# A fixed software-pipelined order for the attention stage, with its weights loaded by casting transfers, in a sigmoid-attention plus feed-forward kernel

**Chip, cores, metric.** One core of a Trainium2 chip. The metric is the device time of one launch in microseconds (us); lower is better. Every time below is a median of fast runs unless said otherwise.

## The reference

```
scores = q @ k.T / sqrt(64) - log(448)            # 8 batches, 12 heads, 448 tokens, head size 64
x = (sigmoid(scores) @ v), heads put side by side  # 3584 tokens x 768
h = x @ w_in                                       # 768 -> 2048
out = (h * sigmoid(beta * h)) @ w_out              # 2048 -> 768
```

No softmax: each score goes through a sigmoid alone, so attention is two matrix products with an elementwise function between.

## The kernel before

Weights are staged in float32 and cast on VectorE at the start. Then 48 units (a batch and a pair of heads) of attention, written in plain order; the framework's scheduler decides the order on each engine. Names: `qn`, `kn`, `vn` as loaded; `tpq`, `tpk` transposes in PSUM; `scc` scores in PSUM, `at2` sigmoids, `av` values in PSUM, `xT` the result.

```python
for c in range(CK):                          # first weights; w_out the same way, 16 pieces
    stage = spool.tile([128, FF], FP32, ...)
    nc.sync.dma_start(out=stage, in_=moe_w_in[c * 128:(c + 1) * 128, :])
    nc.vector.tensor_copy(out=w_in_sb[c], in_=stage)
for b in range(B):
    for hp in range(NHP):
        ...                                  # load qn, kn (GpSimd, casting to fp16), vn (Sync)
        nc.vector.tensor_copy(out=vnh, in_=vn)
        for c in range(NC):                  # 4 transposes of q, copy; then 4 of k, copy
            nc.tensor.transpose(tpq[:, c, :], qn[:, c, :, :], ident)
        ...
        for c in range(NC):                  # two matmuls on the two halves of the array's rows
            scc = sc_ps_pool.tile([SC, 2, 512], FP32, ...)           # two buffers
            for hh in range(2):
                nc.tensor.matmul(out=scc[:, hh, :S], lhsT=kT[lo:lo + 64, c, :], rhs=qT[lo:lo + 64, :], ...)
            nc.scalar.activation(out=at2[:, :, c, :], in_=scc[:, :, :S], func=SIG, ...)
        av = av_ps_pool.tile([128, 2, 512], FP32, ...)               # one buffer
        for c in range(NC):                  # two matmuls on the two halves of its columns
            for hh in range(2):
                nc.tensor.matmul(out=av[lo:lo + 64, hh, :S], lhsT=vnh[:, hh, c, :], rhs=at2[:, hh, c, :], ...)
        for hh in range(2):
            nc.vector.tensor_copy(out=xT_sb[hp][lo:lo + 64, ...], in_=av[lo:lo + 64, hh, :S])
# then the feed-forward stage, unchanged: hps matmuls, sigmoid, product, ops matmuls, store
```

Of the kernel before, what the change touches and what calls it, by code (L numbers as in the profile page):

```python
# [15 lines left out]
def kernel(  # L16
# [10 lines left out]
    nc = tc.nc  # L27
# [27 lines left out]
    with nc.allow_non_contiguous_dma("beta gather"):  # L55
        nc.sync.dma_start(out=beta_sb, in_=moe_beta.rearrange("(m p) -> p m", p=128))

    xT_sb = [wpool.tile([128, NT], FP16, name=f"xT{c}", tag=f"xT{c}")
             for c in range(CK)]

    with tc.tile_pool(name="stage", bufs=2) as spool:
        w_in_sb = []
        for c in range(CK):
            stage = spool.tile([128, FF], FP32, name="wi_stage", tag="wi_stage")
            nc.sync.dma_start(out=stage, in_=moe_w_in[c * 128:(c + 1) * 128, :])
            t = wpool.tile([128, FF], FP16, name=f"w_in_sb{c}", tag=f"wi{c}")
            nc.vector.tensor_copy(out=t, in_=stage)
            w_in_sb.append(t)
        w_out_sb = []
        for m in range(MF):  # L70
            stage = spool.tile([128, DM], FP32, name="wo_stage", tag="wo_stage")
            nc.sync.dma_start(out=stage, in_=moe_w_out[m * 128:(m + 1) * 128, :])
            t = wpool.tile([128, DM], FP16, name=f"w_out_sb{m}", tag=f"wo{m}")
            nc.vector.tensor_copy(out=t, in_=stage)
            w_out_sb.append(t)

        with tc.tile_pool(name="a_sb", bufs=2) as apool, \
                tc.tile_pool(name="tp_ps", bufs=1, space=bass.MemoryType.PSUM) as tp_ps_pool, \
                tc.tile_pool(name="sc_ps", bufs=2, space=bass.MemoryType.PSUM) as sc_ps_pool, \
                tc.tile_pool(name="av_ps", bufs=1, space=bass.MemoryType.PSUM) as av_ps_pool:  # L80
            for b in range(B):
                for hp in range(NHP):
                    h0 = 2 * hp
                    qn = apool.tile([SC, NC, 2, D], FP16, name="qn", tag="qn")
                    kn = apool.tile([SC, NC, 2, D], FP16, name="kn", tag="kn")
                    vn = apool.tile([SC, 2, NC, D], FP32, name="vn", tag="vn")
                    for t, src in ((qn, q), (kn, k)):
                        nc.gpsimd.dma_start(  # L88
                            out=t,
                            in_=src[b, h0:h0 + 2].rearrange(  # L90
                                "hh (p j) d -> p j hh d", j=NC),
                        )
                    nc.sync.dma_start(
                        out=vn,
                        in_=v[b, h0:h0 + 2].rearrange("hh (p j) d -> p hh j d",
                                                      j=NC),
                    )
                    vnh = apool.tile([SC, 2, NC, D], FP16, name="vnh", tag="vnh")
                    nc.vector.tensor_copy(out=vnh, in_=vn)
                    qT = apool.tile([128, S], FP16, name="qT", tag="qT")  # L100
                    kT = apool.tile([128, NC, SC], FP16, name="kT", tag="kT")
                    tpq = tp_ps_pool.tile([128, NC, SC], FP16, name="tpq", tag="tpq")
                    for c in range(NC):
                        nc.tensor.transpose(tpq[:, c, :], qn[:, c, :, :], ident)  # L104
                    nc.vector.tensor_copy(  # L105
                        out=qT.rearrange("f (p c) -> f c p", c=NC), in_=tpq)
                    tpk = tp_ps_pool.tile([128, NC, SC], FP16, name="tpk", tag="tpk")
                    for c in range(NC):
                        nc.tensor.transpose(tpk[:, c, :], kn[:, c, :, :], ident)  # L109
                    nc.vector.tensor_copy(out=kT, in_=tpk)  # L110
                    at2 = apool.tile([SC, 2, NC, S], FP16, name="at2",
                                     tag="at2", bufs=2)
                    for c in range(NC):
                        scc = sc_ps_pool.tile([SC, 2, 512], FP32, name="scc",
                                              tag="scc")
                        for hh in range(2):
                            lo = hh * 64
                            nc.tensor.matmul(  # L118
                                out=scc[:, hh, :S],
                                lhsT=kT[lo:lo + 64, c, :],  # L120
                                rhs=qT[lo:lo + 64, :],
                                start=True, stop=True,
                            )
                        nc.scalar.activation(  # L124
                            out=at2[:, :, c, :], in_=scc[:, :, :S], func=SIG,
                            bias=neglog[:SC], scale=scale,
                        )
                    av = av_ps_pool.tile([128, 2, 512], FP32, name="av",
                                         tag="av")
                    for c in range(NC):  # L130
                        for hh in range(2):
                            lo = hh * 64
                            nc.tensor.matmul(  # L133
                                out=av[lo:lo + 64, hh, :S],
                                lhsT=vnh[:, hh, c, :],
                                rhs=at2[:, hh, c, :],
                                start=(c == 0), stop=(c == NC - 1),
                            )
                    for hh in range(2):
                        lo = hh * 64  # L140
                        nc.vector.tensor_copy(  # L141
                            out=xT_sb[hp][lo:lo + 64, b * S:(b + 1) * S],
                            in_=av[lo:lo + 64, hh, :S])

    with tc.tile_pool(name="m_sb", bufs=2) as mpool, \
            tc.tile_pool(name="g_sb", bufs=2 * MF) as gpool, \
            tc.tile_pool(name="h_ps", bufs=2, space=bass.MemoryType.PSUM) as h_ps_pool, \
            tc.tile_pool(name="o_ps", bufs=2, space=bass.MemoryType.PSUM) as o_ps_pool:
        for g in range(NG):
            t0 = g * TGRP  # L150
            gts = []
            for m in range(MF):
                hps = h_ps_pool.tile([128, NTC, 512], FP32, name="hps", tag="hps")
                for c in range(CK):
                    for n in range(NTC):
                        nc.tensor.matmul(  # L156
                            out=hps[:, n, :S],
                            lhsT=w_in_sb[c][:, m * 128:(m + 1) * 128],
                            rhs=xT_sb[c][:, t0 + n * S:t0 + (n + 1) * S],
                            start=(c == 0), stop=(c == CK - 1),  # L160
                        )
                sg = mpool.tile([128, NTC, S], FP32, name="sg", tag="sg")
                nc.scalar.activation(  # L163
                    out=sg, in_=hps[:, :, :S], func=SIG,
                    bias=0.0, scale=beta_sb[:, m:m + 1],
                )
                gt = gpool.tile([128, TGRP], FP16, name="gt", tag="gt")
                nc.vector.tensor_tensor(  # L168
                    out=gt.rearrange("p (n x) -> p n x", x=S),
                    in0=hps[:, :, :S], in1=sg, op=mybir.AluOpType.mult,  # L170
                )
                gts.append(gt)
            for tt in range(TT):
                ops = o_ps_pool.tile([128, DM], FP32, name="ops", tag="ops")
                for m in range(MF):
                    st = gts[m][:, tt * 128:(tt + 1) * 128]
                    nc.tensor.matmul(out=ops[:, 0:512], lhsT=st,  # L177
                                     rhs=w_out_sb[m][:, 0:512],
                                     start=(m == 0), stop=(m == MF - 1))
                    nc.tensor.matmul(out=ops[:, 512:DM], lhsT=st,  # L180
                                     rhs=w_out_sb[m][:, 512:DM],
                                     start=(m == 0), stop=(m == MF - 1))
                osb = mpool.tile([128, DM], FP32, name="osb", tag="osb")
                nc.scalar.copy(out=osb, in_=ops)  # L184
                nc.sync.dma_start(
                    out=out[t0 + tt * 128: t0 + (tt + 1) * 128, :], in_=osb)
# [30 lines left out]
```

## Time and profile before

| | before |
|---|---|
| time | 585.02 us (583.67 to 587.31) |
| attention, until the first `hps` matmul | 283.2 us of a span of 582.5 |
| one unit in mid-attention | 5.46 us |
| feed-forward | 299.2 us |
| TensorE / ScalarE busy | 95% / 48% |

The prediction shows the lines these come from. In a line of the page's groups, the columns are line, engine, operation, tiles and shapes, count, busy us and mean ns of one, then idle time before and what ended most of it.

### The profile page before, as it was taken

The page shows a single profiled execution, that of the slowest core. Times are in us where ns is not written, and L with a number is a line of the kernel's source. Part 1 is how long each engine was busy: PE and PEld are TensorE (multiplying, and loading weights), DVE is VectorE, ACT ScalarE, POOL GpSimd, SP SyncE. Part 2 cuts the span into 40 slices and gives each one's busy share as a digit, 9 for nine tenths or more (in the row PEclk, how much of TensorE's full clock was granted, in tenths as well). Part 3 has the DMA queues.
Part 4 walks back from the last instruction along what each step waited for, and adds up shares of the span by engine and source line. Part 5 has one row for each costly group of instructions (what it writes and reads, how often), then busy time and mean ns, then how long its engine had stood idle before and what let it go on. Part 6 is the DMA issues. An engine that isn't in the chain of part 4 may idle for free.

```text
span 582.5 us, 6912 instructions
## 1 busy us (share of the span) xinstructions
PE 554.1 (95%) x2816; PEld 255.2 (44%) x2816; DVE 232.9 (40%) x328; ACT 277.7 (48%) x285; POOL 111.4 (19%) x102
## 2 busy tenths in 40 slices
PE   1479999999999999999999999999999999999996
PEld 0233333333333333333355555555655556555564
DVE  2678755555555555555344101441004410044100
ACT  1456776776776776777544112441124421244211
POOL 5425443344344344340000000000000000000000
PEclk9999999999999999999999999999999999999999
DMA  9999977977977977972000111001120001200022
GB/s 251 335 259 217 199 79 81 95 76 83 96 78 81 94 78 82 95 79 34 0 1 0 55 73 64 1 1 55 55 82 0 1 36 73 82 0 1 28 81 82
DMA packets 108367, 46.07 MB, mean 79 GB/s; under 512 B 91184, under 2 KB 101936, under 8 KB 107568
## 3 DMA queue, kind: packets, MB, share of 16 engines
q0 software_dynamic: 87552, 11.02, 29.7%
q1 hardware_dynamic: 20784, 34.62, 18.0%
q8 instruction: 22, 0.36, 0.3%
q14 instruction: 9, 0.07, 0.0%
HBM read 45.62 MB, written 11.01 MB: 97 GB/s over the span
## 4 chain that ended last, share of the span: by engine, by line
PE 93%; DMA 5%; issue 1%; DVE 1%; ACT 0%; POOL 0%; POOLq 0%; ACTq 0%
PE hps L156 26%; PE av L133 18%; PE scc L118 17%; PE ops L177 17%; PE ops L180 8%; PE tpk L109 4%; PE tpq L104 4%; DMA qn<-in_q_dram 3%; DMA kn<-in_k_dram 2%; DVE xT L141 1%; ACT at L124 0%; ACT osb L184 0%; POOL qn L88 0%; POOL ident masks.py:197 0%; POOLq L88 0%
## 5 line engine op out<-in xcount | busy, mean ns | idle before, releaser
L124 ACT ACTIVATE at<-scc,neglog 112x896 f16<-112x896 f32 x192 | 189.5, 1007 | 90.9 <-PE scc L118 82.0
L156 PE MATMUL hps<-xT,w_in_sb 128*128 128x448 f16 x768 | 149.7, 353 | 0.0
L177 PE MATMUL ops<-w_out_sb,gt 128*128 128x512 f16 x448 | 145.8, 379 | 0.0
L168 DVE TENSOR_TENSOR gt<-hps,sg 128x896 f16<-128x896 f32 x64 | 69.9, 1092 | 189.3 <-ACT sg L163 189.3
L180 PE MATMUL ops<-w_out_sb,gt 128*128 128x256 f16 x448 | 122.1, 273 | 0.0
L118 PE MATMUL scc<-qT,kT 64*112 64x448 f16 x384 | 117.9, 615 | 3.4 <-ACT at L124 3.1
L133 PE MATMUL av<-at,vnh 112*64 112x448 f16 x384 | 115.9, 580 | 0.6 <-DVE xT L141 0.4
L156 PEld LDWEIGHTS <-w_in_sb 128*128 128x128 f16 x768 | 74.8, 98 | 74.2 <-issue 6.9
L163 ACT ACTIVATE sg<-hps,beta_sb 128x896 f32<-128x896 f32 x64 | 64.5, 1007 | 86.8 <-PE hps L156 86.8
L141 DVE CAST xT<-av 64x448 f16<-64x448 f32 x96 | 59.7, 622 | 67.7 <-PE av L133 67.1
L184 ACT COPY osb<-ops 128x768 f32<-128x768 f32 x28 | 22.4, 799 | 122.6 <-PE ops L180 122.6
L88 POOL DMA_DIRECT2D qn<-in_q_dram x48 | 56.4, 1175 | 123.7 <-PE tpq L104 110.7
L105 DVE COPY qT<-tpq 128x448 f16<-128x448 f16 x48 | 55.4, 1153 | 36.2 <-PE scc L118 36.1
L118 PEld LDWEIGHTS <-kT 64*112 64x112 f16 x384 | 32.5, 166 | 80.3 <-issue 79.5
L177 PEld LDWEIGHTS <-gt 128*128 128x128 f16 x448 | 43.8, 98 | 52.6
L88 POOL DMA_DIRECT2D kn<-in_k_dram x48 | 58.2, 1213 | 25.4 <-PE tpk L109 17.9
L133 PEld LDWEIGHTS <-vnh 112*64 112x64 f16 x384 | 29.5, 141 | 53.7 <-issue 52.9
L180 PEld LDWEIGHTS <-gt 128*128 128x128 f16 x448 | 43.8, 98 | 5.6
L104 PE MATMUL tpq<-ident,qn 112*128 112x112 f16 x192 | 26.9, 294 | 16.9 <-DMA qn<-in_q_dram 16.4
L109 PE MATMUL tpk<-ident,kn 112*128 112x112 f16 x192 | 35.0, 294 | 3.0 <-DMA kn<-in_k_dram 2.9
L104 PEld LDWEIGHTS <-qn 112*128 112x128 f16 x192 | 15.6, 132 | 34.6 <-DMA qn<-in_q_dram 17.5
L109 PEld LDWEIGHTS <-kn 112*128 112x128 f16 x192 | 17.6, 131 | 21.6 <-issue 16.9
(13 smaller groups left out, 61.3 us busy)
## 6 DMA issues: line engine op xcount, KB each, us to landing
vn<-in_v_dram SPq DMA_DIRECT2D x48, 224.0 KB, 3.0
out_dram<-osb SPq DMA_DIRECT2D x28, 384.0 KB, 2.3
wi_stage<-in_moe_w_in_dram SPq DMA_DIRECT2D x6, 1024.0 KB, 6.6
wo_stage<-in_moe_w_out_dram SPq DMA_DIRECT2D x16, 384.0 KB, 4.1
qn<-in_q_dram POOLq DMA_DIRECT2D x48, 112.0 KB, 3.5
kn<-in_k_dram POOLq DMA_DIRECT2D x48, 112.0 KB, 4.2
beta_sb<-in_moe_beta_dram SPq DMA_DIRECT2D x1, 8.0 KB, 3.0
```

Source lines behind the costliest of these rows:

```text
L88: nc.gpsimd.dma_start(out=t, in_=src[b, h0:h0 + 2].rearrange("hh (p j) d -> p j hh d", j=NC),)
L104: nc.tensor.transpose(tpq[:, c, :], qn[:, c, :, :], ident)
L109: nc.tensor.transpose(tpk[:, c, :], kn[:, c, :, :], ident)
L118: nc.tensor.matmul(out=scc[:, hh, :S], lhsT=kT[lo:lo + 64, c, :], rhs=qT[lo:lo + 64, :], start=True, stop=True,)
L124: nc.scalar.activation(out=at2[:, :, c, :], in_=scc[:, :, :S], func=SIG, bias=neglog[:SC], scale=scale,)
L133: nc.tensor.matmul(out=av[lo:lo + 64, hh, :S], lhsT=vnh[:, hh, c, :], rhs=at2[:, hh, c, :], start=(c == 0), stop=(c == NC - 1),)
L141: nc.vector.tensor_copy(out=xT_sb[hp][lo:lo + 64, b * S:(b + 1) * S], in_=av[lo:lo + 64, hh, :S])
L156: nc.tensor.matmul(out=hps[:, n, :S], lhsT=w_in_sb[c][:, m * 128:(m + 1) * 128], rhs=xT_sb[c][:, t0 + n * S:t0 + (n + 1) * S], start=(c == ...
L163: nc.scalar.activation(out=sg, in_=hps[:, :, :S], func=SIG, bias=0.0, scale=beta_sb[:, m:m + 1],)
L168: nc.vector.tensor_tensor(out=gt.rearrange("p (n x) -> p n x", x=S), in0=hps[:, :, :S], in1=sg, op=mybir.AluOpType.mult,)
L177: nc.tensor.matmul(out=ops[:, 0:512], lhsT=st, rhs=w_out_sb[m][:, 0:512], start=(m == 0), stop=(m == MF - 1))
L180: nc.tensor.matmul(out=ops[:, 512:DM], lhsT=st, rhs=w_out_sb[m][:, 512:DM], start=(m == 0), stop=(m == MF - 1))
```

## The change

The intent: keep TensorE on a fixed order in which transposes run two units early and values one unit late, load three units ahead, and take the weights out of the start. GpSimd loads the weights during attention with transfers that cast, so the staging and 22 casts on VectorE go. The values of both heads share one PSUM tile of 128 x 512 (two buffers), so one copy of 128 partitions takes the place of two of 64 (622 ns each before).

```diff
+    with ..., tc.manual_schedule(engines={mybir.EngineType.PE, mybir.EngineType.Pool}):
+        load(0); load(1); load(2)
+        transposes(0); transposes(1)
+        for n in range(NI):
+            scores(n, 0)
+            values(n - 1, (0, 1))
+            scores(n, 1)
+            transposes(n + 2)
+            load(n + 3)
+            scores(n, 2)
+            values(n - 1, (2, 3))
+            scores(n, 3)
+            if n % 6 == 5 and n // 6 < CK:
+                nc.gpsimd.dma_start(out=w_in_sb[c], in_=moe_w_in[...])     # 1 MB, casts
+        values(NI - 1, (0, 1, 2, 3))
+        for m in range(MF):
+            nc.gpsimd.dma_start(out=w_out_sb[m], in_=moe_w_out[...])
-    # staging of w_in and w_out over Sync, 22 casts on VectorE
-    # the loops over b and hp shown above
```

## The prediction

> **What bounds the kernel now.** I read the page's busy row, slices and chain, then the busy time by stage, then the chain in a window of the middle, then the timeline of single runs of matmuls.

> From the page:

> ```profile
> PE 554.1 (95%) x2816; PEld 255.2 (44%) x2816; DVE 232.9 (40%) x328; ACT 277.7 (48%) x285; POOL 111.4 (19%) x102
> ...
> PE hps L156 26%; PE av L133 18%; PE scc L118 17%; PE ops L177 17%; PE ops L180 8%; PE tpk L109 4%; PE tpq L104 4%; DMA qn<-in_q_dram 3%; DMA kn<-in_k_dram 2%; DVE xT L141 1%; ACT at L124 0%; ACT osb L184 0%; POOL qn L88 0%; POOL ident masks
> ...
> L124 ACT ACTIVATE at<-scc,neglog 112x896 f16<-112x896 f32 x192 | 189.5, 1007 | 90.9 <-PE scc L118 82.0
> L118 PE MATMUL scc<-qT,kT 64*112 64x448 f16 x384 | 117.9, 615 | 3.4 <-ACT at L124 3.1
> L133 PE MATMUL av<-at,vnh 112*64 112x448 f16 x384 | 115.9, 580 | 0.6 <-DVE xT L141 0.4
> L141 DVE CAST xT<-av 64x448 f16<-64x448 f32 x96 | 59.7, 622 | 67.7 <-PE av L133 67.1
> ```

> The chain is TensorE nearly throughout. The kernel has two stages: attention (48 units, each one batch and a pair of heads) until 283.2 us, then the feed-forward part. Stages (the columns are length, busy time and count by engine, granted clock, DMA share, GB/s):

> ```profile
> 60.00:258.00 198.00, 198.00 (x874) 69.79 (x871) 112.60 (x186) 143.48 (x146) 81.90 (x72) 1.00 0.85 92
> 283.20:582.40 299.20, 294.82 (x1666) 162.47 (x1664) 71.12 (x66) 86.85 (x92) 0.00 (x0) 1.00 0.10 38
> ```

> The second stage is 299.2 us of dense matmuls and the change leaves it alone. In the middle of the first, TensorE is never idle, ScalarE is 143/198 = 72% busy. One unit there, in the chain of that window (start, length, what):

> ```profile
> 150.39 0.55 PE scc L118 x2
> 150.94 0.51 PE av L133
> 151.45 0.55 PE scc L118 x2
> 152.00 1.26 PE av L133 x5
> 153.26 0.55 PE scc L118
> 153.81 0.49 PE tpq L104 x4
> 154.30 0.09 PE tpk L109
> 154.39 0.51 PE av L133 x2
> 154.90 0.55 PE scc L118 x2
> 155.45 0.40 PE tpk L109 x3
> 155.85 0.55 PE scc L118
> ```

> One unit lasts 155.85-150.39 = 5.46 us. The order in which the scheduler put the work is poor: nine changes of kind, and the eight value matmuls are cut 1, 5, 2, so that two of them run without their partner.

> How fast is a matmul? From the timeline of TensorE:

> ```profile
> 31.71 0.62 PE L118 MATMUL scc<-qT,kT 64*112 64x448 f16 x2
> 32.26 1.71 PE L133 MATMUL av<-at,vnh 112*64 112x448 f16 x8
> ```

> Two matmuls of half-array shape start 3 to 6 ns apart in the instruction records and run together, but a pair takes (1.71-0.58)/3 = 377 ns (0.58 is the length of one; from the starts 370). That is 448 columns at 1.2 per ns. In the second stage the same 448 columns take 189 ns from start to start; its first three starts, at 283.25, 283.60 and 283.97, are still some 370 apart, and from 284.34 on it is 189. So attention runs at half clock, although the row of granted clock shows 9 everywhere; the clock record has no entry before 284.36 us, so I trust the tempo.

> [...] the half clock of attention, the switch at 284.36 us and the fall at 581.32 us, which is 87 x 3.413 us later. [...] The trace: score pair to value 0.55 us against 0.37 for value pair to pair, so 0.18 us lost; value to score 0.51, so 0.14. [...] The trace: in the first 10 us the q packets (128 B) trickle between 8 KB packets of the weights, and the first q lands 9.5 us after its issue against a median of 3.5.

> **The change part by part.** (1) Fixed order on TensorE: S V V S T S V V S for a unit (S one score pair, VV two value pairs, T eight transposes), with values one unit late and transposes two units early. At half clock, from the intervals above: three S with a change of mode 3 x 0.55; one S followed by S 0.41 (the interval at 37.3 us); two VV 2 x (0.37+0.51) = 1.76; T 7 x 0.093 + 0.23 = 0.88. Sum 4.70 us against 5.46. The gain of 0.76 is two missing singles' slots and three mode changes. Does ScalarE keep up? Four activations back to back took 3.89 us, so 0.97 each. The tight place is S behind S, where the score buffer must be free: it comes 1.84 us after the S two before it, and that one's activation ends 0.72+1.01 = 1.73 after it. It just fits, so TensorE remains the bound.

> (2) Start. No weights ahead of q, k and v. GpSimd issues 0.85 to 1.5 us apart, landing 3.5 later: q and k of unit 0 at about 6, of unit 1 at 8, of unit 2 at 10 us. The built order on VectorE puts three casts of v before the cast of the identity, so transposes wait for the third v, about 6.3, plus 3 x 0.43: first transpose about 7 us (10.8 before). Transpose buffers are single, so each set waits for 1.15+0.41 us of copies; first S about 10, first activation 10.7 (13.84 before), unit 1 begins about 13.3. In the kernel before, only about 6.7 units were done by 60 us (36.3 of the 48 fit in 60 to 258, five come after), where 11 would fit at 5.46: 23 us lost on weights and start, now about 9.

> (3) Moved off the path: the value copies, one 128-partition copy (0.63, estimate from the 0.62 row) for two, and the 22 weight casts, leave VectorE at 0.43+1.15+0.41+0.63 = 2.6 us a unit; it was not the bound. Weights as casting DMAs from GpSimd: 6.3 MB of the first matrix spread over units 5 to 35; the second after the last load, some 20 to 30 us of transfers, wanted only 16 x 2.3 = 36 us into the second stage. Hidden. (1 MB took 6.6 us in the kernel before, and loads run three units ahead.)

> Sum for attention: 13.3 + 45 x 4.70 + 2 x 3.9 (last two units have no transposes and go at ScalarE's pace) + 2 (last activation and values) = 234.6, against 283.2: 48.6 saved, 585.3-48.6 = 536.7 us.

> **The rivals.** (a) The clock is released in attention. Then TensorE's unit is near 2.5 us, ScalarE is the bound at 3.89, and attention is 13 + 47 x 3.93 + 2 = 200, the total 502 to 510. What speaks for it: streaming fills 8 x 373 + 8 x 93 = 3.73 of 4.70 us, 79%, and up to 81% in a window of 3.413 us. Laid on the windows counted back from 284.36 us, attention before reached 79% without release (76% without transposes; the new order would reach 80), and the window that did release it held 87%, the last third with full-array matmuls. The new order falls just into the unknown gap at its low end. I choose one chance in three[...]. A late or broken release lies between 505 and 535. (b) The new place of the wait: if the score buffer comes 0.1 us late, each unit loses that, 48 x 0.1 = 5 us, so 542. (c) DMA becomes the bound. The share of 0.85 looks near full, but in bursts the q and k packets run at a share of 2.0 to 2.4, so one transfer of 912 packets needs about 0.9 us, and a unit with v about 2.5 of 4.7. A MB of weights in the same queue adds about 3 to 6 us six times, against three units of slack. It would give 545 to 560; I hold it unlikely. (d) No gain because the feed-forward stage has to wait for its weights: up to 15 us, 550; unlikely by the sizes in (3).

> **Range and chances.** Without release 537 with 6 either way, two in three; with it 503 to 530, one in three. The middle of that mixture is about 534; a tenth on either side leaves 504 to 545. Faster by over 2% (below 573.6) is nearly sure: 0.97; within 2% 0.02; slower 0.01.

> **What would show it.** Right: in mid-attention a unit of 4.7 us, TensorE without idle time, pairs still 370 ns apart, the value matmuls in fours; ScalarE idle about 0.8 us a unit behind scores; first activation near 11 us; feed-forward 299 us. Rival (a): 448 columns in 189 ns during attention, an entry in the clock record well before the second stage, activations back to back, TensorE idle waiting for them. Rival (b): scores waiting for ACT at half clock. Rival (c): transposes waiting for q or k. Rival (d): ops or hps matmuls waiting for weights. The prediction falls if a unit takes over 5 us at half clock, or if the second stage changes by more than 3 us.

## The result, and the profile after

| | before | changed |
|---|---|---|
| time | 585.02 us (16 runs) | 489.41 us (486.95 to 491.72, 9 runs) |
| ratio of fast runs | 1 | 0.8356, 95% interval 0.8338 to 0.8373 |
| first `hps` matmul | 283.2 us | 186.8 us |
| feed-forward | 299.2 us | 298.6 us |
| one unit in mid-attention | 5.46 us | 3.59 us |

A ratio is the mean of one kernel's fast runs over that of the other's of the same rounds, so it is not quite the ratio of the medians quoted. The time lies 15 us below the low end of the stated range. All of the gain is in attention.

The page of the changed kernel, chain and groups:

```profile
PE 63%; ACT 34%; DMA 1%; issue 1%; DVE 1%; SPq 0%; ACTq 0%
...
L119 ACT ACTIVATE at<-scc,neglog 112x896 f16<-112x896 f32 x192 | 173.0, 1219 | 11.1 <-PE scc L116 11.1
L116 PE MATMUL scc<-qT,kT 64*112 64x448 f16 x384 | 77.8, 382 | 24.2 <-ACT at L119 23.8
L133 PE MATMUL av<-at,vnh 112*64 112x448 f16 x384 | 56.0, 371 | 0.5 <-ACT at L119 0.5
```

ScalarE is now a third of the chain; before it had none. Its idle time before the sigmoids fell from 90.9 us to 11.1. One score matmul shows as 382 ns where it took 615, one value matmul as 371 where it took 580: TensorE itself got faster. The change did nothing to these instructions, so the clock did. The stages (length, busy us and count of PE, PEld, DVE, ACT, POOL, then clock, DMA share, GB/s):

```profile
60.00:180.00 120.00, 102.87 (x800) 46.97 (x799) 74.54 (x133) 120.00 (x135) 79.57 (x80) 1.00 1.33 152
186.80:485.20 298.40, 294.21 (x1665) 162.33 (x1664) 70.50 (x65) 86.86 (x92) 0.00 (x0) 1.00 0.10 38
```

In mid-attention ScalarE is busy 120.00 of 120 us; it is the bound. The timeline of TensorE shows where the clock was let go:

```profile
18.52 0.96 PE L133 MATMUL av<-at,vnh 112*64 112x448 f16 x4
19.41 0.99 PE L116 MATMUL scc<-qT,kT 64*112 64x448 f16 x4
20.34 0.96 PE L133 MATMUL av<-at,vnh 112*64 112x448 f16 x4
21.23 0.62 PE L116 MATMUL scc<-qT,kT 64*112 64x448 f16 x2
21.78 0.37 PE L101 MATMUL tpq<-ident,qn 112*128 112x112 f16 x4
...
22.28 0.40 PE L116 MATMUL scc<-qT,kT 64*112 64x448 f16 x2
```

Four transposes took 0.56 us until then and 0.37 from 21.78 on; a score pair 0.62 and then 0.40. The clock record agrees: its first entry, a full clock, starts at 21.77 us (284.36 in the kernel before). And a unit in the steady state:

```profile
101.11 0.40 PE L116 MATMUL scc<-qT,kT 64*112 64x448 f16 x2
101.43 0.57 PE L133 MATMUL av<-at,vnh 112*64 112x448 f16 x4
102.00 0.40 PE L116 MATMUL scc<-qT,kT 64*112 64x448 f16 x2
102.90 0.40 PE L116 MATMUL scc<-qT,kT 64*112 64x448 f16 x2 [0.50 <-ACT at L119]
```

TensorE idles 0.5 us a unit, waiting for an activation to free a score buffer. This is the prediction's rival (a), with ScalarE faster than I had it.

### The profile page after: what moved, and what is told of

The parts are those of the page before. It is cut to its first block, busy times and chain, and to the rows that moved or that the text cites.

```text
span 485.3 us, 6872 instructions
## 1 busy us (share of the span) xinstructions
PE 446.6 (92%) x2816; PEld 231.5 (48%) x2816; DVE 180.6 (37%) x258; ACT 261.2 (54%) x285; POOL 123.1 (25%) x124
## 4 chain that ended last, share of the span: by engine, by line
PE 63%; ACT 34%; DMA 1%; issue 1%; DVE 1%; SPq 0%; ACTq 0%
ACT at L119 34%; PE hps L178 31%; PE ops L199 20%; PE ops L202 10%; DMA vn<-in_v_dram 1%; PE scc L116 1%; PE av L133 0%; PE tpq L101 0%; DVE vnh L106 0%; PE tpk L101 0%; DVE qT L102 0%; SPq L86 0%; ACT osb L206 0%; DVE ident L51 0%; SPq L56 0%
## 5 line engine op out<-in xcount | busy, mean ns | idle before, releaser
L119 ACT ACTIVATE at<-scc,neglog 112x896 f16<-112x896 f32 x192 | 173.0, 1219 | 11.1 <-PE scc L116 11.1
L185 ACT ACTIVATE sg<-hps,beta_sb 128x896 f32<-128x896 f32 x64 | 64.5, 1007 | 86.1 <-PE hps L178 86.1
L116 PE MATMUL scc<-qT,kT 64*112 64x448 f16 x384 | 77.8, 382 | 24.2 <-ACT at L119 23.8
L82 POOL DMA_DIRECT2D kn<-in_k_dram x48 | 73.3, 1543 | 0.1
L133 PE MATMUL av<-at,vnh 112*64 112x448 f16 x384 | 56.0, 371 | 0.5 <-ACT at L119 0.5
L139 DVE CAST xT<-av 128x448 f16<-128x448 f32 x48 | 29.5, 615 | 6.9 <-PE av L133 6.9
L101 PE MATMUL tpq<-ident,qn 112*128 112x112 f16 x192 | 18.5, 221 | 9.7 <-DVE ident L51 8.9
L133 PEld LDWEIGHTS <-vnh 112*64 112x64 f16 x384 | 13.8, 109 | 20.8 <-issue 20.7
L106 DVE CAST vnh<-vn 112x512 f16<-112x512 f32 x48 | 21.6, 451 | 5.7 <-DMA vn<-in_v_dram 5.3
L101 PEld LDWEIGHTS <-qn 112*128 112x128 f16 x192 | 10.8, 100 | 19.8 <-issue 12.8
L104 DVE COPY kT<-tpk 128x448 f16<-128x448 f16 x48 | 19.7, 411 | 0.0
```

The lines of the kernel that those rows point to most:

```text
L82: nc.gpsimd.dma_start(out=t, in_=src[b, h0:h0 + 2].rearrange("hh (p j) d -> p j hh d", j=NC))
L101: nc.tensor.transpose(tp[:, c, :], src2[:, c, :, :], ident)
L116: nc.tensor.matmul(out=scc[:, hh, :S], lhsT=s["kT"][lo:lo + 64, c, :], rhs=s["qT"][lo:lo + 64, :], start=True, stop=True)
L119: nc.scalar.activation(out=s["at2"][:, :, c, :], in_=scc[:, :, :S], func=SIG, bias=neglog[:SC], scale=scale)
L133: nc.tensor.matmul(out=s["av"][lo:lo + 64, :S], lhsT=s["vnh"][:, hh, c, :], rhs=s["at2"][:, hh, c, :], start=(c == 0), stop=(c == NC - 1), ...
L139: nc.vector.tensor_copy(out=xT_sb[hp][:, b * S:(b + 1) * S], in_=s["av"][:, :S])
```

## The experiments

For all of these I use one measure, the **streaming share** of a window. The recorded clock changes of a run lie whole multiples of 3.413 us apart: 87 in the kernel before (284.36 to 581.32 us), 136 in the changed one (21.77 to 485.98), and, to the 0.1 us quoted below, 8 in the kernel before with a burst (72.8 to 100.1), 4 in the scheduler's order with a burst (28.9 to 42.5), 2 and then 3 in the run with the other start (4.25, 11.1, 21.3). So I lay windows of that length back and forth from these changes; the spacing is all that was measured of them. In them I take the time in which columns stream, from the starts in the instruction records. A half-array matmul counts half, so a score or value pair that runs together (starts 3 to 6 ns apart) counts once, and transposes count whole. All 2816 matmuls of both kernels are in the records. I assume that 448 columns stream for 0.373 us at half clock (a pair took 0.370 to 0.377) and half of that at full clock (0.189 measured from start to start), from the recorded start on, and a transpose for 0.093 and 0.047 (0.093 and 0.049 from start to start), so a share is an estimate.

### A burst in the kernel before

```diff
+                    if b * NHP + hp == 8:
+                        warm = av_ps_pool.tile([128, 2, 512], FP32, name="warm", tag="av")
+                        for i in range(20):
+                            nc.tensor.matmul(out=warm[:, i % 2, :S], lhsT=w_in_sb[0][:, 0:128],
+                                             rhs=w_in_sb[0][:, 128:128 + S], start=True, stop=True)
```

> The kernel before, with 20 useless full-array matmuls of 448 columns put once into unit 8 of 48 (outputs unchanged). Theory 1, the half clock was what held attention and its order of work only failed to release it: the clock is released in or just after the burst (near 65 us), stays released, and from there the old order runs at ScalarE's pace, about 3.6 to 3.9 us a unit instead of 5.46; total 510 to 530. Theory 2, the fixed order itself is the gain (the old order is slow by its waits whatever the clock): units after the burst stay above 5 us, total 580 to 592.

Measured: 584.58 us over all 20 runs (583.76 over the 15 fast ones), ratio 0.9983 (0.9958 to 1.0008). Neither theory came true as written, though the total lies in the range of the second. The clock was released at 72.8 us, and taken back at 100.1 us, for the rest of attention. The stages while released and after:

```profile
82.40:91.30 8.90, 6.69 (x51) 2.96 (x50) 7.52 (x11) 7.62 (x9) 4.62 (x5) 1.00 0.96 104
105.60:143.80 38.20, 38.20 (x169) 13.47 (x168) 21.30 (x35) 27.73 (x29) 15.80 (x15) 0.50 0.83 85
```

The first stretch holds two units (4.45 and 4.43 us by the starts of their first scores), the second seven of 5.46. So at full clock the old order costs 4.4 us, not 3.6: it is held by its waits. TensorE's timeline in that stretch:

```profile
86.58 0.35 PE L142 MATMUL av<-at,vnh 112*64 112x448 f16 x1 [0.45 <-DVE xT L150]
86.86 0.40 PE L118 MATMUL scc<-qT,kT 64*112 64x448 f16 x2
87.19 0.76 PE L142 MATMUL av<-at,vnh 112*64 112x448 f16 x5
87.87 0.40 PE L118 MATMUL scc<-qT,kT 64*112 64x448 f16 x2
88.92 0.36 PE L104 MATMUL tpq<-ident,qn 112*128 112x112 f16 x4 [0.65 <-DVE qT L105]
```

The single `av` buffer waits for its copies and the single transpose buffer for its copy. The gain of those few units about paid for the burst. (Nine of the 20 runs show a mean clock below 0.83, against 0.841 in the profiled one, and took 587.4 to 589.1 us: by that mean some 15 us less at full clock, an estimate; no trace of them was kept.) And the old order gives the clock back: the last window before that had a share of 0.355, and TensorE was busy for 13.18 of the 17.60 us from 82.4 to 100 us. (This clock column is right only because the record has entries here: 0.50 after 100 us, the tempo of the kernel before, where the same column shows 1.00 for want of entries.)

### The change without its fixed order

```diff
-            tc.tile_pool(name="av_ps", ...) as av_ps, \
-            tc.manual_schedule(engines={mybir.EngineType.PE, mybir.EngineType.Pool}):
+            tc.tile_pool(name="av_ps", ...) as av_ps:    # the scheduler orders TensorE and GpSimd
```

> The changed kernel without the fixed order: the scheduler orders TensorE again, and does it as S V S V S V T5 S V T3, each value pair alone, ten changes of kind a unit. Theory 1 (density decides the clock): about 5.2 us a unit at half clock, a share of streaming of 0.57 in matmuls and 0.71 with transposes, so no release in attention; attention about 12 + 48 x 5.2 = 262, total 558 to 570. Theory 2 (the start without stalls, or something else of the change, releases the clock): release within the first 40 us and a total within 10 us of the changed kernel, 485 to 500.

Measured: 563.88 us, ratio 0.9623, theory 1. A unit took 5.24 us, and the first clock entry is at 264.9 us, in the feed-forward stage. From 60 to 250 us, before that entry (so the clock column says nothing), TensorE is always busy:

```profile
60.00:250.00 190.00, 190.00 (x872) 66.17 (x870) 86.58 (x146) 146.33 (x147) 79.22 (x75) 1.00 0.83 95
```

So the start, the loads and the single value copy alone are worth 21 us, and they release nothing.

### The fixed order without the new weight loading

```diff
-            if n % 6 == 5 and n // 6 < CK:
-                nc.gpsimd.dma_start(out=w_in_sb[c], ...)      # and the loop for w_out
+    # staging and casts of the kernel before, ahead of the attention loop
```

> The fixed order of the changed kernel, but the weights brought in as in the kernel before (staged at the start, cast on VectorE). Theory 1: the clock is released too, but only when the stalls of the first 40 us are over; total 505 to 520, i.e. 15 to 30 us above the changed kernel, all of it in the first 60 us. Theory 2 (a start without stalls is needed for the release): no release, total about 555 to 565.

Measured: 517.38 us, ratio 0.8822, theory 1. Released at 45.9 us, lost twice while VectorE, which also copies for attention, waited for staged weights (9.5 us of such waits between 46 and 77 us), and held from 76.7 us. Before the release two units ran without a stall at half clock, from 36.3 us: 4.67 us each, against the 4.70 predicted. From 83.2 to 200 us ScalarE is always busy, as in the changed kernel:

```profile
83.20:200.00 116.80, 100.49 (x786) 46.15 (x785) 72.06 (x130) 116.80 (x131) 71.53 (x63) 1.00 1.19 127
```

So the change without its weight loading is worth 68 us, the change without its fixed order 21, the whole 96. (The first still has the loads three units ahead, the second `av` buffer and the single value copy, so it is not the order alone; those parts are in the second too.)

### One group of values cut in two, without and with a burst

```diff
+            values(n - 1, (0,))
             scores(n, 0)
-            values(n - 1, (0, 1))
+            values(n - 1, (1,))
             scores(n, 1)
```

> The changed kernel with one of the two groups of four value matmuls cut in two (two more changes of kind, nothing else). At half clock a unit should take about 5.0 us and stream 3.73/5.0 = 0.745 of it, between the 0.71 of the scheduler's order, which was never released, and the 0.79 of the changed kernel, which was released in its first full window. If the line lies where the windows so far put it[...]: not released, or only late; total 530 to 555. If it is lower: released within 40 us, total 488 to 495.

Measured: 550.80 us, ratio 0.9419. Units took 4.99 us, and there was no release before the feed-forward stage. Two more changes of kind a unit, on engines that otherwise do the same, cost 61 us against the changed kernel. Nor is it chance from run to run: the four runs lie between 550.46 and 551.41 us, those of the changed kernel between 486.95 and 491.72. Then the same order with the burst (20 matmuls before unit 3):

> The split order that took 550.8 us and was never released in attention, fixed as it is, plus 20 useless full-array matmuls once before unit 3 (the burst in the scheduler's order proved nothing, since its transposes and loads were moved too and a late q emptied a window). If release and hold have two lines[...], one burst is enough: released near 30 us, held at 3.6 us a unit with a share of 0.53 to the end, total 489 to 497. If the clock follows the density of the moment: back at half clock within a few windows, 548 to 560.

Measured: 494.12 us, ratio 0.8433. The clock was released at 27.9 us and held to the end of the feed-forward stage, with units of 3.59 us. The stages in the columns used above, without the burst first and with it second (the first has no clock entry yet, so its clock column says nothing):

```profile
60.00:240.00 180.00, 180.00 (x868) 65.19 (x866) 103.48 (x146) 145.26 (x145) 87.41 (x88) 1.00 0.98 116
```

```profile
60.00:180.00 120.00, 107.21 (x808) 55.46 (x807) 75.25 (x133) 120.00 (x135) 80.03 (x76) 1.00 1.34 152
```

TensorE always busy and ScalarE at 81% in the first; ScalarE always busy in the second. This pair shows that the state of the clock is worth this much: one order, 57 us apart by a burst of useless work. The burst itself cost some 5 us (its unit took 10.2 from scores to scores, against 4.99).

### The burst in the scheduler's order

The same burst of 20 matmuls before unit 3, in the kernel without the fixed order.

> The changed kernel with the scheduler's order (563.9 us, never released in attention) plus 20 useless full-array matmuls in unit 3. Theory 1, the fixed order matters because it releases the clock[...]: at full clock this order runs at ScalarE's pace of 3.56 us with a share near 0.53, so it holds from about 30 us to the end; total 488 to 505. Theory 2, the scheduler's order cannot run at ScalarE's pace even at full clock, as the kernel before could not (4.42 us a unit, then it fell back): it falls back or stays above 4.2 us a unit; total 525 to 570.

Measured: 566.66 us, ratio 0.9690. Released at 28.9 us, lost at 42.5. This settles nothing about the order: the scheduler had moved transposes and loads around the burst, a q landed late, TensorE waited 3.7 us for it, and that window's share was 0.11. Two units before the stall took 3.57 and 3.91 us by their first activations. Whether this order would hold the clock without a stall stays open.

### Half the sigmoids

```diff
-                out=s["at2"][:, :, c, :], in_=scc[:, :, :S], func=SIG,
+                out=s["at2"][:, 0, c, :], in_=scc[:, 0, :S], func=SIG,
-                        rhs=s["at2"][:, hh, c, :],
+                        rhs=s["at2"][:, 0, c, :],
```

> The changed kernel, but ScalarE takes the sigmoid of one head of each pair only and both heads' value matmuls read that one (wrong result on purpose; TensorE's work is the same). If ScalarE bounds attention once the clock is released: activations come about 0.5 us apart, a unit falls from 3.59 us to TensorE's own 2.9, total 455 to 462, and TensorE is without idle time. If something else paces the units (buffers, DMA, VectorE): the unit stays above 3.4 us, total over 480.

Measured: 477.65 us (two runs), ratio 0.8154. The result is wrong; the record marks it correct all the same, so its check does not see such an error. Part of the expectation came true: where nothing stalled, TensorE had no idle time and a unit took 2.77 us (from 29.43 to 32.20 between the same group of values). The shortest interval of two activations was 0.532 us; the others in such a unit were 0.59 to 0.83, as ScalarE now waited for scores. So ScalarE was the bound. But the total missed by 16 us: the next limit is right behind. From the chain between 20 and 131 us:

```profile
27.22 0.93 POOL w_in_sb L159
28.15 8.96 DMA qn<-in_q_dram
...
67.12 1.16 POOL w_in_sb L159
68.28 10.30 DMA qn<-in_q_dram
```

When a 1 MB casting transfer went into GpSimd's queue, the q issued next took 6.2 to 10.3 us to land (six cases; the median of all q is 5.2). In the changed kernel it took 6.9 to 8.5 (median 4.2); at 3.59 us a unit, three units of slack hide this, at 2.77 they don't. TensorE stalls, the clock drops (from 38.7, 79.6, 100.1 and 124.0 us) and comes back later.

### An attempt at the start

```diff
-    nc.vector.tensor_copy(out=ident, in_=ident32)
+    nc.scalar.copy(out=ident, in_=ident32)          # and 18 matmuls on a constant tile before load(0)
```

> The changed kernel with the identity cast on ScalarE (no wait for the casts of v) and 18 useless matmuls from the first microsecond on. If the late identity and the half clock of the first units are what the start still costs: first transpose near 7 us instead of 8.86, clock released before the first scores, saving 1.7 + about 2.5 us: 483 to 487 against 489. If the rest of the start is bound by the landing of q and k: within 1 us of the changed kernel.

Measured: 489.18 us, ratio 0.8368, no gain. The clock was released at 4.25 us and lost at 11.1, in the waits of the first units; it returned at 21.3, about as in the changed kernel. The first transpose came at 6.99 us instead of 8.86, but TensorE then waited 1.54 us for k until 8.90 and 1.52 for another k until 13.88, and unit 2 began no earlier. So what bounds the start is mainly the landing of q and k. This run also lost the clock at the end of attention, from 181.7 to 188.6 us, after a window with a share of 0.408. That cost it little: its first activation of unit 24 was already 1.0 us behind the changed kernel's, its first `hps` matmul 1.65.

### ScalarE on 128 partitions

Cut at 112 keys, each activation uses 112 of 128 partitions; one of 896 columns took 1.01 us on 112 (the page before) and 1.01 on 128 (the run below). This version cuts the 448 keys of a head as 3 x 128 and puts the last 64 of both heads into one matmul with block-diagonal weights; one transfer a batch brings those keys, two those values. q's transposed copy is written straight and the value copy does the reordering. The first weights come in halves.

```diff
+            if c == KJ:                              # last 64 keys of both heads
+                nc.tensor.matmul(out=scc[:, 0, :S], lhsT=s["kbd"], rhs=s["qT"], ...)
+                nc.scalar.activation(out=s["at3"], in_=scc[:, 0, :S], func=SIG, ...)
+                return
-                    lhsT=s["kT"][lo:lo + 64, c, :],                     # c of 4, 112 keys
+                    lhsT=s["kT"][lo:lo + 64, c * 128:(c + 1) * 128],    # c of 3
```

> The changed kernel with the keys cut as 3 x 128 per head and the last 64 of both heads together (block-diagonal weights), so ScalarE uses 128 partitions instead of 112: three activations of 896 columns and one of 448 a unit, 3 x 0.890 + 0.532 = 3.20 us instead of 3.56; first weights in halves. If ScalarE is the only bound: 48 x 0.36 = 17 us less, 470 to 476. If GpSimd's issuing (2.8 us for q and k) and the waits behind casting weight transfers come in the way: 476 to 487.

Measured: correct by the check, 478.32 us (477.74 to 478.53), ratio 0.8177 (0.8164 to 0.8189). The fastest version not made wrong, 2.1% below the changed kernel by the two ratios. Units took 3.32 us instead of 3.59; I had expected 3.20, but the activation of 448 columns took 0.632 us until the next one began, not the 0.532 put in, and one of the three others 0.906, not 0.890. The start cost 3 us more. With the identity cast moved to ScalarE here too:

> The 128-partition version with the identity cast on ScalarE instead of behind VectorE's clears and casts. First activation was at 15.06 us, 2.9 later than in the changed kernel, because the identity came at 11.5; now transposes should begin at 7 to 9 us and the total fall by 2 to 4 us: 474 to 477. If q, k or the single transpose buffers bound the start: within 1 us of 478.3.

Measured: 478.25 us, ratio 0.8160, no gain: transposes began at 5.7 us, but k kept TensorE waiting 4.4 us in all and the first activation came at 16.1.

## Why the prediction was wrong

**What held.** The bound of the kernel before (TensorE, by its order), its half clock in attention, and the cost of the new order at half clock: 4.70 us worked out, 4.71 measured on unit 1 of the changed kernel and 4.67 on two units of the order-only run. Feed-forward unchanged: 298.6 against 299.2. Loads and weights were hidden, so rivals (c) and (d) did not come: after the first q, TensorE's weight loads and matmuls waited 0.2 us in all for transfers. The direction and the mechanism of rival (a), with its signs: early clock entry, activations back to back, TensorE waiting for them.

**The first step that failed: "I choose one chance in three" for the release.** The sum of 536.7 us follows TensorE at half clock to the end of attention. The clock was released at 21.8 us, and from then on a unit took 3.59 us at ScalarE's pace instead of 4.70 at TensorE's. The low chance rested on a count. I laid windows over the kernel before and found 79% without release, just under the new order's 79 to 81. But I counted the two lone value matmuls of a unit as full, and each uses half of the array (112*64 in the records). Counted by half, the kernel before tops at 0.775, and the window just before its release held 0.82. The larger fault was to set the peak windows of the old order beside the mean of the new one: even counted in full, the old order's windows average only 0.75 between 60 and 245 us. The kernels line up by their mean share in a steady unit at half clock (8 x 0.373 + 8 x 0.093 = 3.73 us of streaming over the unit):

| order | unit at half clock | share | released in attention |
|---|---|---|---|
| before | 5.46 us | 0.683 | no |
| scheduler's, with the new start | 5.24 us | 0.711 | no |
| fixed, one group cut | 4.99 us | 0.747 | no |
| fixed | 4.70 us | 0.793 | yes, at 21.8 us |

Single windows do not sort so clearly. In the changed kernel the release came after the second of two windows that both hold 0.766; in the order with one group cut, 26 of 68 windows between 15 and 245 us hold 0.766 to 0.779 without release; in the order-only run there were windows of up to 0.82 without release. One that did end in a release there held 0.59 of matmuls and 0.22 of transposes; without the transposes it would lie below many that did not. I could not make it sharper by shifting the windows or weighting the transposes. So the runs show that the denser order is released and the less dense ones are not; that this share decides it is not shown. The clock was lost after windows with lower shares: in the kernel before with a burst it was kept after one with 0.369 and lost after one with 0.355, and in the run with the other start it was lost after one with 0.408 at the end of attention. The released new order has (8 x 0.187 + 8 x 0.047)/3.59 = 0.52, an estimate, above all of these. And one order was seen in both states: the one with a group cut stayed at half clock without a burst, at 0.747, and at full clock after it, at 0.52. My rival (a) put all its units at ScalarE's pace, so it took for granted that a released clock stays; that was my estimate, and I gave the rival too little weight.

**The second step that failed: ScalarE's pace, 0.97 us an activation.** I divided the length of four in a row, 3.89 us, by four. Its three intervals were 1.005, 0.906 and 0.975 us, because scores came late, and length over count is no interval at all. Rows of two and three in the kernel before give the pace:

```profile
13.84 1.91 ACT L124 ACTIVATE at<-scc,neglog 112x896 f16<-112x896 f32 x2 [11.60 <-PE scc L118]
20.76 2.81 ACT L124 ACTIVATE at<-scc,neglog 112x896 f16<-112x896 f32 x3 [5.01 <-PE scc L118]
```

One takes 1.007, so 1.91 - 1.007 = 0.90 and (2.81 - 1.007)/2 = 0.90 from start to start. The changed kernel has a median of 0.890, hence the 3.59 us. The term "47 x 3.93" is 16 us too long; with 47 x 3.59, rival (a) comes to 13 + 169 + 2 + 299 = 483, and to some 485 with the 1.8 us between span and device time (an estimate; 489 measured). So the range failed even for the rival that came true. TensorE's own unit at full clock, "near 2.5 us" in the prediction, was 2.77 in the half-sigmoid run; ScalarE's 3.59 hid that miss.

**The start** was a little worse than predicted: first transpose 8.86 (7), first activation 12.12 (10.7), unit 1 at 15.1 (13.3). The casts of v took up to 0.7 us each, and the identity, after them, 0.72. It was not what decided the result.

**Where the 96 us went.** An estimate from units: the order saves 5.46 - 4.70 = 0.76 us a unit at half clock, 36 us over 48; the release a further 4.70 - 3.59 = 1.11, 50 over the 45 units after it. The start: the kernel before has four units done at 44.0 us, 22 late by its own pace of 5.46; the changed one has three done at 23.8, 10 late by 4.70; 12 saved. The sum is 98 against 96.5 measured to the first `hps` matmul (the last units, without transposes, are shorter in both). The orders at half and full clock (old 5.46 and 4.43, new 4.70 and 3.59) show that both parts count: at full clock the old order was held by its waits on single buffers, and in the burst run it did not keep the clock. How much of this is the order and how much the second `av` buffer and the single value copy was not separated.

## What to carry to other kernels

Check the tempo of matmuls against their column count before trusting a clock row (the row of the kernel before shows 9 throughout, while 448 columns took 370 ns in attention and 189 in most of the feed-forward stage), and if a stage runs at half clock, count its streaming share as a mean over the steady unit, not by its peak windows. Here a slightly denser order (0.793 against 0.747), or one burst of useless work in an order that then kept the clock at a share of 0.52, gained about a fifth of the stage. Take an engine's pace from start to start, not as length over count. Where a stage has become bound by ScalarE, look at how many partitions its instructions fill: in the version that fills 128 in place of 112 a unit took 3.32 us instead of 3.59.
